# A linear-attention layer and two feed-forward layers on one core: low parts of the weights and r*k move from GpSimd to VectorE, raw chunks and attention inputs get three buffers, and the first block's gl is issued one slot part later

## The chip, the cores and the metric

The kernel runs on one core of a Trainium2 chip. The metric is the device time of one execution in microseconds, the median of three runs. Engines are named as in the profile: PE is TensorE, DVE is VectorE, ACT is ScalarE, POOL is GpSimd, SP is SyncE, which only issues transfers (SPq is its queue).

## The reference

Float32 throughout: 4 batches, 8 heads, 768 tokens, 48 channels a head. A recurrent attention makes x, then two feed-forward layers follow, each with a squared ReLU in the middle.

```python
def _attn_ref(r, k, v, w, u):
    state = np.zeros((B, H, D, D)); y = np.zeros_like(r)
    for t in range(S):
        kt, vt, rt, wt = (k[:, :, t], v[:, :, t], r[:, :, t], w[:, :, t])
        cur = np.einsum('bhd,bhe->bhde', u[None] * kt, vt)
        y[:, :, t] = np.einsum('bhd,bhde->bhe', rt, state + cur)
        state = wt[:, :, :, None] * state + np.einsum('bhd,bhe->bhde', kt, vt)
    return y

def _moe_ref(x, w_in, w_out):        # (3072, 384) @ (384, 2048), (3072, 2048) @ (2048, 384)
    h = x @ w_in
    g = np.maximum(h, 0.0) ** 2
    return g @ w_out

# reference: x = attention, tokens by channels; _moe_ref with w_in, w_out; _moe2_ref the same with its own weights
```

## The kernel before

**Products in high and low parts.** Every feed-forward product is made of three float32r products: an operand is split into a rounded high part and the rest (whi and wlo of the weights, xh and xl of x, gh and gl of the activation), and high times high, high times low and low times high are added up in PSUM.

**Slots.** Each layer goes over 7 blocks of tokens (512, 256, 256, then four of 512; in the second layer the two short ones come last), and in a block over 16 chunks f of the 2048 hidden channels. One block and one chunk make a slot; `slots` lists all 224 in order. The loop at the end of `chunked` issues for slot s, in this order: `emit_h` (nine products into h), `between(s, 0)`, `square` (ReLU and square on ScalarE), `emit_out(s - 2)` (the products of the slot two back into acc), `between(s, 1)`, `split` (gh, then gl = g - gh on VectorE). In the first block gh is made by ScalarE, later by VectorE. The schedule is manual: every engine works through its instructions in the order in which this program issues them, and semaphores hold an instruction until its operands are there and its buffer is free. A slot part is one of the two calls of `between`.

**Weights.** `Weights` turns the packed weights into whi and wlo, one chunk (128x768) at a time, 16 chunks a layer. `load` brings a raw chunk of 768 KB by SyncE's queue. `pieces` is a generator, and each call of `piece` issues one piece of it: clamp, shift, top, tail (VectorE), then whi (ScalarE) and wlo (GpSimd); ScalarE's absolute value of the next chunk (`magnitude`, `c<-raw`) is issued behind top, the load of a further raw chunk behind tail. Raw chunks have two buffers, and so have the converted words c. In the first block each slot issues three pieces in part 0 and two in part 1, and so converts the chunk that is needed two slots later. Chunks of the second layer are converted from the last block of the first layer on, at 1.6 pieces a slot part (TICKS).

**Attention.** 24 tiles of 128 tokens, each in seven steps (`Attn.steps`): 0, two scans on VectorE (G and F) and r*k on GpSimd; 1, k*G and r*F on VectorE and, on ScalarE, the squares of G and F for a range check; 2, transposes and scores on TensorE, copies on ScalarE; 3, the masked scores (ScalarE, GpSimd); 4, the state (TensorE, VectorE, ScalarE; GpSimd scales v); 5, the output y; 6, its transpose, split into xh and xl. For the first 6 tiles r*k is taken from the tile wkr (112 x 512, channels by time), for the others from rk, tokens by channels, which has a load of its own. Inputs of a tile (wkr with w, k, r, 676 KB; vn and sv) have two buffers and are loaded by SyncE's queue: wkr when step 2 of the tile two before has been issued, vn and sv behind its step 5.

**START.** Tiles 0 to 3 make the first block's x. The string START orders their steps by hand: a digit is the next step of that tile, `w` is one piece of the weights, `x` four products that nothing reads (`keep_warm`), `l` the two first raw loads. Tiles 4 and 5 have their steps in the slots of the first block (`spread`), and so on, a block ahead.

Of the kernel before, what the change touches and what calls it, by code (L numbers as in the profile page):

```python
# [19 lines left out]
T = 128  # L20
# [17 lines left out]
RAW_BUFS = 2  # L38
# [4 lines left out]
START = "lxx000x1110w1w0xw1w02w12x021323xww23w23ww23w3w3x"  # L43
# [8 lines left out]
class Attn:  # L52
# [6 lines left out]
    def __init__(self, ctx, tc, wkr, nat, u, ub, ps):  # L59
# [11 lines left out]
        self.chk = cp.tile([QR, 2 * NTILE], F32, name="chk")  # L71
# [10 lines left out]
    def load_wkr(self, i):  # L82

        if i >= NTILE:
            return
        nc = self.nc
        wkr = self.ld.tile([QR, WKR], F32, tag="wkr", name="wkr")
        rk = self.ld.tile([T, 2, H * D], F32, tag="rk", name="rk")
        cuts = (0, SW + 1, SW + 513, WKR) if i < 1 else (0, WKR)
        for lo, hi in zip(cuts, cuts[1:]):  # L90
            nc.sync.dma_start(out=wkr[:, lo:hi], in_=self.wkr_d[i, :, lo:hi])
        if i >= SUMMED_BY_PE:
            nc.sync.dma_start(out=rk, in_=self.nat_d[i, :, 0:2])
        self.wkr_t[i] = wkr, rk
# [13 lines left out]
    def load_u(self):  # L108
        self.nc.sync.dma_start(out=self.ub, in_=self.ub_d)
# [5 lines left out]
    def steps(self, i, xdst):  # L115
# [13 lines left out]
        G = self.wp1.tile([QR, SW + 1], F32, tag="G", name="G")  # L129
        F = self.wp1.tile([QR, SW + 1], F32, tag="F", name="F")  # L130
# [9 lines left out]
        r, k = rk[:, 0], rk[:, 1]  # L140
        if by_pe:
            rkT = rk.rearrange("q n d -> q (n d)")[0:QR, 0:SEG * C].rearrange("q (s t) -> q s t", s=SEG)
            nc.gpsimd.tensor_tensor(out=rkT, in0=rT, in1=kS, op=ALU.mult)
        else:
            nc.gpsimd.tensor_tensor(out=r, in0=r, in1=k, op=ALU.mult)
# [4 lines left out]
        for n, t in enumerate((G, F)):  # L150
            nc.scalar.activation(out=t[:, 1:], in_=t[:, 1:], func=AF.Square, accum_out=self.chk[:, 2 * i + n:2 * i + n + 1])
# [117 lines left out]
class Weights:  # L269


    def __init__(self, ctx, tc, packed):
# [8 lines left out]
        self.gen = None  # L281

    def load(self):
# [5 lines left out]
        self.nc.sync.dma_start(out=raw, in_=self.packed[k // KF][k % KF].bitcast(I32).rearrange("p (m w) -> p m w", w=2))  # L289
        self.raw[k] = raw  # L290

    def piece(self, end=2 * KF):

        if self.gen is None and self.begun < end:
            self.gen = self.pieces()
        if self.gen is not None and next(self.gen, 0) == 0:
# [6 lines left out]

    def pieces(self):
        nc = self.nc
# [5 lines left out]
        conv.clamp()  # L311
        yield
# [8 lines left out]
        yield  # L321
        hi, lo = self.hl[k // KF, k % KF] = tuple(self.p.tile([128, 2 * DM], F32R, tag=t, name=t) for t in ("whi", "wlo"))
        nc.scalar.copy(out=hi, in_=conv.cf)  # L323
# [403 lines left out]
```

## Time and profile before

| | us |
|---|---|
| median of three runs (lowest to highest) | 1020.34 (1018.11 to 1020.72) |
| the profiled execution | 1018.85 |
| its span, first to last instruction | 1017.0 |
| busy in the span: TensorE | 951.3 |
| VectorE | 547.3 |
| ScalarE | 473.2 |
| GpSimd | 167.2 |

The profile is one execution, read by the hardware's profiler. A row of the trace gives an instruction's engine, line, tiles, shape and duration, and the idle time of its engine before it with what ended that. Busy time is a sum over an engine's instructions. The clock is the share of full speed that was granted to TensorE: at 1.00 it runs at 2.4 GHz, at 0.5 at 1.2 GHz, and values between are a mix in time.

### The profile page before, as it was taken

How to read it: one execution, taken by the hardware profiler on the slowest of the kernel's cores; microseconds unless marked ns; L12 is line 12 of the kernel's file. 1: busy time of each engine (PE TensorE's matmuls, PEld its weight loads, DVE VectorE, ACT ScalarE, POOL GpSimd, SP SyncE). 2: the span in 40 equal slices, each digit the busy share in tenths (PEclk: the TensorE clock that was granted, in tenths of full speed). 3: DMA queues.
4: the chain of work that ended last, by engine and by line, in shares of the span. 5: the costliest groups of instructions: out<-in, count | busy, mean ns of one | idle time of the engine just before them, and what ended most of it. 6: DMA issues, size and time to landing. Idle time of an engine off the chain costs nothing.

```text
span 1017.0 us, 16836 instructions
## 1 busy us (share of the span) xinstructions
PE 951.3 (94%) x6708; PEld 830.2 (82%) x6708; DVE 547.3 (54%) x908; ACT 473.2 (47%) x923; POOL 167.2 (16%) x160
## 2 busy tenths in 40 slices
PE   6577868998999999999999999999999999999997
PEld 6565646898978888888888888999999999999996
DVE  4777667655784574655835898822323223222332
ACT  4344655555655546546454565533333333333442
POOL 2422232230323022121210222300000000000000
PEclk8757888998999999999999999999999999999999
DMA  7242443233224214123102334210010010100100
GB/s 210 91 121 93 136 136 121 83 102 102 81 86 118 79 46 126 56 78 118 32 1 73 134 123 147 84 43 11 11 42 22 14 39 11 37 6 6 47 17 19
DMA packets 28119, 73.82 MB, mean 73 GB/s; under 512 B 3616, under 2 KB 15264, under 8 KB 28032
## 3 DMA queue, kind: packets, MB, share of 16 engines
q1 hardware_dynamic: 28032, 72.66, 22.9%
q8 instruction: 54, 0.88, 0.4%
q14 instruction: 33, 0.27, 0.1%
HBM read 63.21 MB, written 9.44 MB: 71 GB/s over the span
## 4 chain that ended last, share of the span: by engine, by line
PE 64%; DVE 3%; issue 1%; DMA 1%; ACT 1%; ACTq 0%; DVEq 0%; SPq 0%
PE acc L600 30%; PE h L557 30%; PE ab L173 1%; PE ab L216 1%; DMA raw<-in_w_dram 1%; DVE gh L573 1%; DVE c L257 1%; PE ab L189 1%; PE ab L158 0%; PE ab L223 0%; DVE gl L575 0%; DVE c L260 0%; DVE c L266 0%; DVE c L263 0%; PE ab L190 0%
## 5 line engine op out<-in xcount | busy, mean ns | idle before, releaser
L557 PE MATMUL h<-xh,whi 128*128 128x512 f32 (+1 forms) x672 | 251.1, 374 | 16.8 <-ACT whi L323 16.7
L557 PE MATMUL h<-xh,wlo 128*128 128x512 f32 (+1 forms) x672 | 249.1, 371 | 8.1 <-POOL wlo L324 8.1
L557 PE MATMUL h<-xl,whi 128*128 128x512 f32 (+1 forms) x672 | 247.4, 368 | 0.0
L573 DVE CAST gh<-gf 128x512 fp32r<-128x512 f32 (+1 forms) x208 | 87.4, 420 | 296.7 <-PE acc L600 238.4
L565 ACT ACTIVATE gf<-h 128x512 f32<-128x512 f32 (+1 forms) x224 | 119.9, 535 | 272.5 <-PE h L557 270.0
L575 DVE TENSOR_TENSOR gl<-gf,gh 128x512 fp32r<-128x512 f32 (+1 forms) x224 | 161.3, 720 | 45.6 <-ACT gh L573 30.8
L557 PEld LDWEIGHTS h<-xh,whi 128*128 128x128 f32 x672 | 129.2, 192 | 38.3 <-ACT whi L323 19.7
L557 PEld LDWEIGHTS h<-xh,wlo 128*128 128x128 f32 x672 | 129.6, 193 | 32.2 <-POOL wlo L324 12.4
L557 PEld LDWEIGHTS h<-xl,whi 128*128 128x128 f32 x672 | 129.3, 192 | 16.9 <-DVE xl L226 0.3
L566 ACT ACTIVATE gf<-gf 128x512 f32<-128x512 f32 (+1 forms) x224 | 128.1, 572 | 7.1
L600 PE MATMUL acc<-whi,gh 128*128 128x384 f32 x384 | 129.4, 337 | 1.7 <-ACT o L604 1.7
L600 PE MATMUL acc<-gh,whi 128*128 128x512 f32 (+1 forms) x336 | 125.0, 372 | 5.9 <-ACT o L604 5.8
L600 PE MATMUL acc<-whi,gl 128*128 128x384 f32 x384 | 129.4, 337 | 0.0
L600 PE MATMUL acc<-wlo,gh 128*128 128x384 f32 x384 | 129.0, 336 | 0.0
L600 PE MATMUL acc<-gl,whi 128*128 128x512 f32 (+1 forms) x336 | 122.1, 363 | 0.1
L600 PE MATMUL acc<-gh,wlo 128*128 128x512 f32 (+1 forms) x336 | 121.6, 362 | 0.0
L324 POOL TENSOR_TENSOR wlo<-c,whi 128x768 fp32r<-128x768 f32 x32 | 60.9, 1902 | 175.8 <-ACT whi L323 167.2
L600 PEld LDWEIGHTS acc<-gh,whi 128*128 128x128 f32 x336 | 64.7, 193 | 17.9 <-ACT o L604 7.5
L600 PEld LDWEIGHTS acc<-whi,gh 128*128 128x128 f32 x384 | 72.3, 188 | 5.5 <-ACT o L604 2.0
L600 PEld LDWEIGHTS acc<-wlo,gh 128*128 128x128 f32 x384 | 72.2, 188 | 3.4
L600 PEld LDWEIGHTS acc<-gh,wlo 128*128 128x128 f32 x336 | 64.3, 191 | 9.8
L600 PEld LDWEIGHTS acc<-gl,whi 128*128 128x128 f32 x336 | 64.4, 192 | 9.5 <-DVE starts L132 0.3
(70 smaller groups left out, 1020.4 us busy)
## 6 DMA issues: line engine op xcount, KB each, us to landing
raw<-in_w_dram SPq DMA_DIRECT2D x32, 768.0 KB, 4.3
wkr<-in_wkr_dram SPq DMA_DIRECT2D x23, 675.9 KB, 5.1
rk<-in_nat_dram SPq DMA_DIRECT2D x18, 384.0 KB, 5.5
vn<-in_nat_dram SPq DMA_DIRECT2D x24, 192.0 KB, 2.6
sv<-in_nat_dram SPq DMA_DIRECT2D x48, 96.0 KB, 2.6
out_dram<-o SPq DMA_DIRECT2D x24, 192.0 KB, 2.0
x<-o SPq DMA_DIRECT2D x15, 256.0 KB, 2.2
xr<-x SPq DMA_DIRECT2D x12, 256.0 KB, 2.6
```

Source lines behind the costliest of these rows:

```text
L173: nc.tensor.matmul(out=scv[other[a], n, :], lhsT=kS[rows, n, :], rhs=rT[rows, n, :], start=True, stop=True)
L189: nc.tensor.matmul(out=Uv[c][0:64, p, :], lhsT=ksT[rows, p, 0:64], rhs=vn[rows, 2 * p, :], start=True, stop=True)
L216: nc.tensor.matmul(out=y[64 * c:64 * c + 64, D * h:D * h + D], lhsT=rs[rows, a, 2 * p + c, :], rhs=sv[rows, a, 2 * p + c, :], start=True, ...
L257: self.v.tensor_scalar(out=self.cf, in0=self.cf, scalar1=HIGH_WORD_MIN, scalar2=HIGH_WORD_MAX, op0=ALU.max, op1=ALU.min)
L324: nc.gpsimd.tensor_tensor(out=lo, in0=conv.cf, in1=hi.bitcast(F32), op=ALU.subtract)
L557: nc.tensor.matmul(out=h[:, 0:N], lhsT=a[:, cs], rhs=b[:, kk, 0:N], start=n == 0, stop=n == 8)
L565: nc.scalar.activation(out=g[:, 0:N], in_=h[:, 0:N], func=AF.Relu)
L566: nc.scalar.activation(out=g[:, 0:N], in_=g[:, 0:N], func=AF.Square)
L573: (nc.scalar.copy if l == j == 0 else nc.vector.tensor_copy)(out=gh[:, 0:N], in_=g[:, 0:N])
L575: nc.vector.tensor_tensor(out=gl[:, 0:N], in0=g[:, 0:N], in1=gh[:, 0:N].bitcast(F32), op=ALU.subtract)
L600: nc.tensor.matmul(out=dst, lhsT=a, rhs=c, start=f == n == 0, stop=f == KF - 1 and n == 2)
```

## The change

The low part of a chunk, `lo = c - hi`, goes from GpSimd to VectorE. It is no longer issued behind whi but in a function of its own, `cut`, which is called as the second piece of the following chunk (behind that chunk's clamp), or by a call of `piece` that finds no chunk left to begin. The number of pieces a chunk stays five: clamp, cut, shift, top, and tail with whi. `ready` counts a chunk once its low part is issued. Raw chunks get three buffers, all three loaded at the start, the first by ScalarE's queue.

r*k of the first six tiles goes from GpSimd to VectorE, behind the two scans. wkr gets three buffers; it is loaded for the tile three ahead, when step 3 has been issued, and rk, where it is loaded, for the tile two ahead. The first loads change order and queue: wkr of tile 1, ub and the first raw chunk go by ScalarE's queue, wkr of tile 2 is loaded at the start too, uB goes behind the tiles' loads.

In the first block, gl is not issued with gh in `split` but in part 0 of the next slot, behind its pieces (`rests`).

G and F lie in one tile, and one square over both replaces two; the range check has one column a tile. START has a new order: 11 pieces of the weights in place of 12, 9 `x` in place of 7. The scratch space for dynamic transfers is set to 4096.

```diff
--- before.py
+++ after.py
@@ -35,12 +35,14 @@
 RANGE_SQ = 2.0 ** 59
 
 HIGH_WORD_MIN, HIGH_WORD_MAX = 2.0 ** -15, 2.0 ** 16 * (1.875 - 2.0 ** -23)
-RAW_BUFS = 2
+RAW_BUFS = 3
+
+AHEAD = 3
 
 SUMMED_BY_PE = 6
 
 
-START = "lxx000x1110w1w0xw1w02w12x021323xww23w23ww23w3w3x"
+START = "xx000x1101wwx120w2x1w02w103x2w132wx32w3w2x3w3w3x"
 
 LEAD = 2
 
@@ -68,7 +70,7 @@
         self.ident = cp.tile([128, 128], F32, name="ident")
         self.uB = cp.tile([T, H * D], F32, name="uB")
         self.ub = cp.tile([QR, NP, 2], F32, name="ub")
-        self.chk = cp.tile([QR, 2 * NTILE], F32, name="chk")
+        self.chk = cp.tile([QR, NTILE], F32, name="chk")
         self.Sc = {}
         self.wkr_t, self.v_t = {}, {}
 
@@ -79,19 +81,24 @@
         nc.gpsimd.affine_select(out=self.ident, in_=self.ident, pattern=[[-1, 128]], base=0,
                                 channel_multiplier=1, compare_op=ALU.not_equal, fill=1.0)
 
-    def load_wkr(self, i):
+    def load_wkr(self, i, queue=None):
 
         if i >= NTILE:
             return
         nc = self.nc
-        wkr = self.ld.tile([QR, WKR], F32, tag="wkr", name="wkr")
-        rk = self.ld.tile([T, 2, H * D], F32, tag="rk", name="rk")
+        queue = queue or nc.sync
+        wkr = self.ld.tile([QR, WKR], F32, tag="wkr", name="wkr", bufs=AHEAD)
         cuts = (0, SW + 1, SW + 513, WKR) if i < 1 else (0, WKR)
         for lo, hi in zip(cuts, cuts[1:]):
-            nc.sync.dma_start(out=wkr[:, lo:hi], in_=self.wkr_d[i, :, lo:hi])
-        if i >= SUMMED_BY_PE:
-            nc.sync.dma_start(out=rk, in_=self.nat_d[i, :, 0:2])
-        self.wkr_t[i] = wkr, rk
+            queue.dma_start(out=wkr[:, lo:hi], in_=self.wkr_d[i, :, lo:hi])
+        self.wkr_t[i] = wkr, None
+
+    def load_rk(self, i):
+
+        if SUMMED_BY_PE <= i < NTILE:
+            rk = self.ld.tile([T, 2, H * D], F32, tag="rk", name="rk")
+            self.nc.sync.dma_start(out=rk, in_=self.nat_d[i, :, 0:2])
+            self.wkr_t[i] = self.wkr_t[i][0], rk
 
     def load_v(self, i):
         if i >= NTILE:
@@ -106,7 +113,9 @@
         self.v_t[i] = vn, sv
 
     def load_u(self):
-        self.nc.sync.dma_start(out=self.ub, in_=self.ub_d)
+        self.nc.scalar.dma_start(out=self.ub, in_=self.ub_d)
+
+    def load_uB(self):
         self.nc.sync.dma_start(out=self.uB, in_=self.u_d.rearrange("(o h) d -> o (h d)", o=1).to_broadcast([T, H * D]))
 
     def bank(self):
@@ -126,8 +135,8 @@
         def seg(t, o, q=slice(0, QR)):
             return t[q, 1:SW + 1].rearrange("q (s j) -> q s j", s=SEG)[:, :, o:o + C]
 
-        G = self.wp1.tile([QR, SW + 1], F32, tag="G", name="G")
-        F = self.wp1.tile([QR, SW + 1], F32, tag="F", name="F")
+        GF = self.wp1.tile([QR, 2, SW + 1], F32, tag="GF", name="GF")
+        G, F = GF[:, 0], GF[:, 1]
         aend = self.wp.tile([QR, SEG], F32, tag="aend", name="aend", bufs=4)
         nc.vector.memset(self.starts[:, 65::65], 1.0)
         nc.vector.tensor_tensor_scan(out=G[:, 1:][:, ::-1], data0=Wt[:, 1:][:, ::-1], data1=self.starts[:, 1:][:, ::-1],
@@ -137,18 +146,18 @@
         nc.vector.tensor_tensor_scan(out=F[:, 1:], data0=Wt[:, 0:SW], data1=self.starts[:, 0:SW],
                                      initial=0.0, op0=ALU.mult, op1=ALU.add)
         by_pe = i < SUMMED_BY_PE
-        r, k = rk[:, 0], rk[:, 1]
         if by_pe:
+            rk = self.ld.tile([T, 2, H * D], F32, tag="rk", name="rk")
             rkT = rk.rearrange("q n d -> q (n d)")[0:QR, 0:SEG * C].rearrange("q (s t) -> q s t", s=SEG)
-            nc.gpsimd.tensor_tensor(out=rkT, in0=rT, in1=kS, op=ALU.mult)
+            nc.vector.tensor_tensor(out=rkT, in0=rT, in1=kS, op=ALU.mult)
         else:
+            r, k = rk[:, 0], rk[:, 1]
             nc.gpsimd.tensor_tensor(out=r, in0=r, in1=k, op=ALU.mult)
             nc.gpsimd.tensor_tensor(out=r, in0=r, in1=self.uB, op=ALU.mult)
         yield
         nc.vector.tensor_tensor(out=kS, in0=kS, in1=seg(G, 1), op=ALU.mult)
         nc.vector.tensor_tensor(out=rT, in0=rT, in1=seg(F, 0), op=ALU.mult)
-        for n, t in enumerate((G, F)):
-            nc.scalar.activation(out=t[:, 1:], in_=t[:, 1:], func=AF.Square, accum_out=self.chk[:, 2 * i + n:2 * i + n + 1])
+        nc.scalar.activation(out=GF[:, :, 1:], in_=GF[:, :, 1:], func=AF.Square, accum_out=self.chk[:, i:i + 1])
         yield
         kq = self.wp.tile([T, NP * QR + H], F32, tag="ksT", name="ksT")
         ksT, q = kq[:, 0:NP * QR].rearrange("t (p q) -> t p q", p=NP), kq[:, NP * QR:]
@@ -278,22 +287,25 @@
         self.hl = {}
         self.raw = {}
         self.loaded = self.begun = self.ready = 0
-        self.gen = None
-
-    def load(self):
+        self.gen = self.whole = None
+
+    def load(self, queue=None):
         k = self.loaded
         if k >= 2 * KF:
             return
         self.loaded += 1
         raw = self.raw_p.tile([128, 2 * DM, 2], I32, tag="raw", name="raw")
-        self.nc.sync.dma_start(out=raw, in_=self.packed[k // KF][k % KF].bitcast(I32).rearrange("p (m w) -> p m w", w=2))
+        (queue or self.nc.sync).dma_start(out=raw, in_=self.packed[k // KF][k % KF].bitcast(I32).rearrange("p (m w) -> p m w", w=2))
         self.raw[k] = raw
 
     def piece(self, end=2 * KF):
 
-        if self.gen is None and self.begun < end:
+        if self.gen is None:
+            if self.begun == end:
+                self.cut()
+                return
             self.gen = self.pieces()
-        if self.gen is not None and next(self.gen, 0) == 0:
+        if next(self.gen, 0) == 0:
             self.gen = None
             self.piece(end)
 
@@ -301,8 +313,14 @@
         self.conv = ToFloat32(self.nc, self.raw.pop(k), self.tmp_p.tile([128, 2 * DM], I32, tag="c", name="c"))
         self.conv.magnitude()
 
+    def cut(self):
+        if self.whole is not None:
+            conv, hi, lo = self.whole
+            self.nc.vector.tensor_tensor(out=lo, in0=conv.cf, in1=hi.bitcast(F32), op=ALU.subtract)
+            self.whole = None
+            self.ready += 1
+
     def pieces(self):
-        nc = self.nc
         k = self.begun
         self.begun += 1
         if k == 0:
@@ -310,6 +328,8 @@
         conv = self.conv
         conv.clamp()
         yield
+        self.cut()
+        yield
         conv.shift()
         yield
         conv.top()
@@ -318,11 +338,9 @@
         yield
         conv.tail()
         self.load()
-        yield
         hi, lo = self.hl[k // KF, k % KF] = tuple(self.p.tile([128, 2 * DM], F32R, tag=t, name=t) for t in ("whi", "wlo"))
-        nc.scalar.copy(out=hi, in_=conv.cf)
-        nc.gpsimd.tensor_tensor(out=lo, in0=conv.cf, in1=hi.bitcast(F32), op=ALU.subtract)
-        self.ready = k + 1
+        self.nc.scalar.copy(out=hi, in_=conv.cf)
+        self.whole = conv, hi, lo
         yield
 
     def done(self):
@@ -485,10 +503,15 @@
     block_of = [j for j, n in enumerate(BLOCKS[0]) for _ in range(n // T)]
 
     A.load_wkr(0)
+    A.load_wkr(1, nc.scalar)
     A.load_u()
     A.load_v(0)
-    A.load_wkr(1)
+    W.load(nc.scalar)
+    A.load_wkr(2)
     A.load_v(1)
+    A.load_uB()
+    for _ in range(RAW_BUFS - 1):
+        W.load()
     A.consts()
 
     xs = {}
@@ -512,8 +535,9 @@
             gens[i] = A.steps(i, lambda: xdst(i))
         next(gens[i])
         seen[i] += 1
-        if seen[i] == 3:
-            A.load_wkr(i + 2)
+        if seen[i] == 4:
+            A.load_wkr(i + AHEAD)
+            A.load_rk(i + 2)
         elif seen[i] == NSTEP - 1:
             A.load_v(i + 2)
 
@@ -533,10 +557,7 @@
 
     keep_warm(9)
     for what in START:
-        if what == "l":
-            for _ in range(RAW_BUFS):
-                W.load()
-        elif what == "w":
+        if what == "w":
             W.piece()
         elif what == "x":
             keep_warm(4)
@@ -570,10 +591,18 @@
         N = BLOCKS[l][j]
         g = gs[l, j, f]
         gh = g_p.tile([128, 512], F32R, tag="gh", name="gh")
-        (nc.scalar.copy if l == j == 0 else nc.vector.tensor_copy)(out=gh[:, 0:N], in_=g[:, 0:N])
         gl = g_p.tile([128, 512], F32R, tag="gl", name="gl")
-        nc.vector.tensor_tensor(out=gl[:, 0:N], in0=g[:, 0:N], in1=gh[:, 0:N].bitcast(F32), op=ALU.subtract)
         gs[l, j, f] = gh, gl
+        late = l == j == 0
+        (nc.scalar.copy if late else nc.vector.tensor_copy)(out=gh[:, 0:N], in_=g[:, 0:N])
+
+        def rest():
+            nc.vector.tensor_tensor(out=gl[:, 0:N], in0=g[:, 0:N], in1=gh[:, 0:N].bitcast(F32), op=ALU.subtract)
+
+        if late:
+            rests.append(rest)
+        else:
+            rest()
 
     x2 = [dram.tile([128, 3, n], F32, name=f"x2_{j}") for j, n in enumerate(BLOCKS[0])]
     slots = [(l, j, f) for l in range(2) for j in range(len(BLOCKS[l])) for f in range(KF)]
@@ -648,8 +677,9 @@
         if s < L0:
             if j == 0:
                 for _ in range(3 - part):
-                    if W.begun < min(KF, f + LEAD + 1) or W.gen is not None:
-                        W.piece(min(KF, f + LEAD + 1))
+                    W.piece(min(KF, f + LEAD + 1))
+            if part == 0 and rests:
+                rests.pop()()
             if j + 1 < len(BLOCKS[0]):
                 if (f, part) == (0, 0):
                     plan[:] = spread(j + 1, 2 * KF)
@@ -661,6 +691,7 @@
     plan = []
     bad = []
     due = [0]
+    rests = []
     for s in range(total + 2):
         if s < total:
             l, j, f = slots[s]
@@ -714,7 +745,7 @@
     import concourse.bacc as bacc
     from concourse.bass_utils import run_bass_kernel_spmd
 
-    nc = bacc.Bacc("TRN2", target_bir_lowering=False, num_devices=1)
+    nc = bacc.Bacc("TRN2", target_bir_lowering=False, num_devices=1, dynamic_dma_scratch_size=4096)
     arrays, args = {}, []
     for name, a in lay_out(**inputs).items():
         arrays[f"in_{name}_dram"] = a
```

## Rows read from the trace of the kernel before

**Rows 1.** Windows by stage: stretch, length, busy time of each engine, clock, DMA share, GB/s.

```profile
0.00:68.00 68.00, 43.76 (x519) 40.52 (x519) 41.15 (x62) 29.21 (x59) 22.69 (x28) 0.70 0.50 145
68.00:183.00 115.00, 90.26 (x493) 67.95 (x492) 82.89 (x95) 60.76 (x103) 37.24 (x25) 0.84 0.38 123
183.00:302.00 119.00, 111.40 (x1216) 103.03 (x1215) 80.08 (x165) 67.23 (x167) 26.53 (x32) 0.97 0.30 88
302.00:1017.00 715.00, 705.89 (x4485) 618.65 (x4485) 343.20 (x588) 315.98 (x596) 80.75 (x76) 1.00 0.17 55
```

**Rows 2.** Waits of TensorE from 340 us to the end: total, times, longest.

```profile
PE acc L600 <- ACT o L604: 1.7, 1, 1.7
```

**Rows 3.** Timeline of TensorE: the first product of block 0 (start, duration).

```profile
67.94 0.77 PE L557 MATMUL h<-xh,whi 128*128 128x512 f32 x1
```

**Rows 4.** Groups on VectorE, 68 to 183 us: busy, mean ns of one | idle before.

```profile
L575 DVE TENSOR_TENSOR gl<-gf,gh 128x512 fp32r<-128x512 f32 x15 | 26.5, 1764 | 28.1 <-ACT gh L573 28.1
...
L266 DVE SCALAR_TENSOR_TENSOR c<-raw,c 128x768 int32<-128x768 int32 x14 | 13.3, 952 | 0.3
L257 DVE TENSOR_SCALAR c<-c 128x768 f32<-128x768 f32 x13 | 9.5, 728 | 0.0
...
L148 DVE TENSOR_TENSOR wkr<-wkr,G 112x512 f32<-112x512 f32 x2 | 1.4, 686 | 0.0
```

**Rows 5.** Timeline of one slot of block 0, all engines but TensorE.

```profile
126.55 0.96 DVE L266 SCALAR_TENSOR_TENSOR c<-raw,c 128x768 int32<-128x768 int32 x1
...
127.64 0.81 ACT L323 CAST whi<-c 128x768 fp32r<-128x768 f32 x1
128.36 0.62 ACT L573 CAST gh<-gf 128x512 fp32r<-128x512 f32 x1
...
128.53 1.81 POOL L324 TENSOR_TENSOR wlo<-c,whi 128x768 fp32r<-128x768 f32 x1 [4.62 <-ACT whi L323]
...
129.01 1.88 DVE L575 TENSOR_TENSOR gl<-gf,gh 128x512 fp32r<-128x512 f32 x1 [1.50 <-ACT gh L573]
```

**Rows 6.** Timeline at 601 us, second-layer weights: VectorE and GpSimd.

```profile
601.14 0.69 DVE L575 TENSOR_TENSOR gl<-gf,gh 128x512 fp32r<-128x512 f32 x1
...
601.72 1.84 POOL L324 TENSOR_TENSOR wlo<-c,whi 128x768 fp32r<-128x768 f32 x1 [4.42 <-ACT whi L323]
601.75 2.23 DVE L257 TENSOR_SCALAR c<-c 128x768 f32<-128x768 f32 x1
```

**Rows 7.** Timeline of VectorE in START.

```profile
3.86 1.24 DVE L133 TENSOR_TENSOR_SCAN G<-wkr,starts 112x520 f32<-112x520 f32 x1 [2.23 <-DMA wkr<-in_wkr_dram]
...
8.53 0.69 DVE L149 TENSOR_TENSOR wkr<-wkr,F 112x512 f32<-112x512 f32 x1
...
12.91 2.30 DVE L133 TENSOR_TENSOR_SCAN G<-wkr,starts 112x520 f32<-112x520 f32 x1 [3.68 <-DMA wkr<-in_wkr_dram]
...
24.06 0.56 DVE L257 TENSOR_SCALAR c<-c 128x768 f32<-128x768 f32 x1 [5.87 <-ACT c L254]
...
30.82 3.47 DVE L133 TENSOR_TENSOR_SCAN G<-wkr,starts 112x520 f32<-112x520 f32 x1
...
59.02 2.26 DVE L197 TENSOR_TENSOR Sp<-Sn,aend 112x192 f32<-112x192 f32 x1
...
62.07 0.36 DVE L197 TENSOR_TENSOR Sp<-Sn,aend 112x192 f32<-112x192 f32 x1 [0.33 <-ACT sv L202]
```

**Rows 8.** Groups on ScalarE, 68 to 183 us.

```profile
L254 ACT ACTIVATE c<-raw 128x768 f32<-128x768 f32 x14 | 12.9, 922 | 34.2 <-DMA raw<-in_w_dram 29.4 <-POOL wlo L324 4.7
L323 ACT CAST whi<-c 128x768 fp32r<-128x768 f32 x14 | 11.5, 822 | 8.4 <-DVE c L266 6.7 <-DVE starts L132 1.5
```

**Rows 9.** Groups on GpSimd, 68 to 183 us.

```profile
L324 POOL TENSOR_TENSOR wlo<-c,whi 128x768 fp32r<-128x768 f32 x14 | 25.7, 1835 | 75.4 <-ACT whi L323 75.4
```

**Rows 10.** DMA issues on the page: KB each, median us to landing.

```profile
raw<-in_w_dram SPq DMA_DIRECT2D x32, 768.0 KB, 4.3
```

**Rows 11.** Window of six microseconds in block 0, columns as in rows 1.

```profile
84.00:90.00 6.00, 5.75 (x16) 4.18 (x14) 5.79 (x9) 2.07 (x3) 0.90 (x1) 0.60 0.00 0
```

## The prediction

> **What bounds the kernel now.** I read the stage windows first. From 302 us to the end TensorE is busy for 705.9 of 715 us at clock 1.00, and between 183 and 302 for 111.4 of 119 [rows 1]; in the last two thirds it waits once, 1.7 us [rows 2]. Nothing that VectorE, GpSimd or the queues do there can move the end by more than a few microseconds. The time that can be won lies ahead of 183 us: the START order (0 to 68, TensorE busy 43.8, clock 0.70) and block 0 of the first layer (68 to 183, busy 90.3 of 115, clock 0.84) [rows 1]. Since the stages behind are full of TensorE work that depends on nothing but these two, what block 0 ends earlier, the kernel ends earlier.
>
> Next, what holds block 0. Its first product starts at 67.94 [rows 3]. Each slot needs one converted chunk. VectorE is busy for 82.9 us and idle for 32.1 [rows 1]; 28.1 of those 32.1 stand ahead of gl, waiting for ScalarE's gh [rows 4]. The timeline of one slot shows why: tail ends at 127.51, whi runs to 128.45, gh behind it to 128.98, only then gl at 129.01 and, behind gl, the next clamp [rows 5]. So gl, last in its slot, puts VectorE through a ScalarE round trip in every slot. Meanwhile GpSimd's low part runs from 128.53 to 130.34, and gl, begun at 129.01, ends at 130.89, after 1.88 us [rows 5]. The same gl without GpSimd takes 0.69; a clamp begun 0.03 us behind a low part takes 2.23 and ends 0.42 after it [rows 6], where a free one takes 0.56 [rows 7]. I read this as VectorE standing still while GpSimd's low part runs. The mean gl in block 0, 1.764 [rows 4], is thus 1.07 too long. ScalarE besides waits 29.4 us for raw chunks [rows 8], and its whi queues behind that.
>
> **Block 0, summed on VectorE.** From its 82.9 us busy [rows 1]:
> - gl without GpSimd beside it: 15 x (1.764 - 0.69) = -16.1 [rows 4, 6].
> - clamp likewise: 13 x (0.728 - 0.56) = -2.2 [rows 4, 7].
> - The low parts come to VectorE: chunks 1 to 15, 15 instructions. No 128x768 subtraction of VectorE stands in the trace. Between the 512-element gl (0.69, as if size were free) and GpSimd's own 1.835 [rows 9] I take 0.952, that of tail, also 768 elements from two SBUF operands [rows 4]: +14.3. The bounds would make this 10.4 or 27.5.
> - r*k of tiles 4 and 5, 112x512 from SBUF as the product with G: 2 x 0.686 = +1.4 [rows 4].
> - START has one piece less (11 for 12), so the shift of chunk 2 falls here: +0.6, a clamp's time.
>
> That is 80.9 busy. Waits: a low part needs whi, which ends 0.94 us after tail [rows 5]; the next clamp covers 0.58 of it, so 14 x 0.36 = 5.0 remain. gl now runs behind clamp, low part and shift of the next slot, over 2 us after tail, while whi and gh are done 1.47 after it [rows 5]: its 28.1 us go. The other idle time, 32.1 - 28.1 = 4.0, I leave. Sum 89.9. The last low part now comes a piece later than its whi, with products behind it: +2. So 92 for 115, **23 us less**.
>
> Can TensorE follow? 90.3 busy at clock 0.84 [rows 1] is 90.3 x 0.84 = 76 at full clock (an estimate), and at 0.84 itself just under 92. It fits, narrowly.
>
> Raw chunks: a load is issued behind tail of chunk k and takes 4.3 us [rows 10]. With two buffers it is wanted one slot later, with three two slots later; at 92 / 16 = 5.7 us a slot that is 2 x 5.7 - 0.95 = 10.4 us; the 29.4 us wait [rows 8] should vanish. Behind a waiting load on SyncE's queue stand all later ones; a tile's load that waits over 6 us would make one raw chunk late. Since wkr is now loaded one step later for a tile further ahead, it finds its buffer freer. I cost the loads at nothing; uncovered, the bound is the 29.4.
>
> One Square for G and F does the same elements in one instruction less; ScalarE is busy for 60.8 of 115 us [rows 1], so nothing. In START, though, tile 1's scan now waits for both halves, some 0.6 us (estimated from whi, 0.822 for 768 elements [rows 8]).
>
> **Weights of the second layer.** 16 low parts come to VectorE, +0.95 each, and the clamp beside them loses 2.23 - 0.56 = 1.67 [rows 6, 7]. TensorE hides both: it does not wait there [rows 2]. Zero; without the cover, 16 x 0.95 = 15 us.
>
> **START.** Tile 1's scan began at 12.91 after 3.68 us of waiting for its load [rows 7]; that load now stands first on ScalarE's queue instead of ninth on SyncE's. It can begin once tile 0 is done: its last product, begun at 8.53, ended at 9.22 [rows 7]; with its r*k on VectorE (0.69) and its Square (about 1.2) that is 11.1, -1.8. GpSimd's r*k and low parts no longer stretch the scans of tiles 1 and 2 (2.30 and 3.47, against 1.24) and one state product (2.26 against 0.36): -5.2 [rows 7]. VectorE takes on four r*k and a low part and loses a shift: 4 x 0.69 + 0.95 - 0.56 = +3.2. That makes -3.8. The new order puts tile 2's scan right behind the first clamp, where it came 6.8 us later (24.06 to 30.82 [rows 7]); some of this returns as waiting for TensorE, and I take 3 of 6.2. **START: 7 us less**, bounds 2 to 13: the lower without the reordering's 3 and with the delay of the next paragraph, the upper with all of the 6.2 and half of the 5.87 us that the first clamp waited.
>
> Against it: two transfers now start together. At the stage's 145 GB/s [rows 1] the 228 KB of tile 0's first piece (112 partitions of 521 floats) are 1.6 us, the most by which tile 1's load can delay it. The Trainium skill (DMA: Bandwidth & Descriptors, "Issuing engines are not separate DMA queues") speaks against the second queue: transfers of different issuers interleave on the same 16 DMA engines and only issue time is saved. By that, START gains 5.4 and not 7; no row of this trace has two issuers.
>
> **Sum.** 1018.85 (the profiled execution, span 1017.0) - 23 - 7 = **989 us**. The median shown, 1020.34, lies 1.5 above, inside the spread of the three runs.
>
> **Rivals.**
> - *TensorE's clock takes part of it.* At a mean of 0.75, between the 0.70 of START and the 0.84, its work is 76 / 0.75 = 101 us, not 92: 998 us. For it: short waits now come in every slot. Against: while TensorE is slow it is itself late, and waits stop.
> - *The clock stays down all through block 0*, the slower side. At the 0.60 of 84 to 90 us [rows 11], 76 / 0.60 = 127, +12, less START's 7: 1024 us. It decides where 76 / c exceeds 115 + 7, at c under 0.62. Against: that stretch is 6 us of the 115. The Trainium skill (TensorE: Matmul & The Clock Gate, "HAM oscillation") tells of kernels that wait in every iteration and start each one cold; by it this rival would hold, and the 0.84 of block 0 [rows 1] bears it out only in part.
> - *The round trip only moves*, from gl to the low part or to raw chunks behind held loads: half of the 28.1 stays, block 0 gains 9: 1003 us.
> - *Better than the sum.* START gains 12, and whi and leftover waits overlap with attention (5.0 + 4.0), as do two stretched scans (2): 1018.85 - 34 - 12 = 973.
> - *GpSimd isn't what stretches VectorE*: the change would not do what it says. The 18.3 of gl and clamp and the 5.2 of START stay: 1013 us; with low parts at 1.835 another 13, 1026. Against: [rows 6].
>
> **Chances.** Forecast 0.48; clock at 0.75 0.17; round trip moved 0.12; better 0.11; GpSimd innocent 0.05, half of it slower; clock down 0.07, some of it no change. Three runs tell 0.3% from no change here, about 3 us. Faster 0.88, same 0.04, slower 0.08. The forecast's own range is 982 to 996; the range for 8 in 10 reaches to the clock, the moved round trip and the better case: 973 to 1008.
>
> **What would show it.** Right: gl near 0.69 in block 0 and no wait for gh; no long clamps; low parts near 0.95, each behind a wait of some 0.4 for whi; ScalarE's waits for raw gone; tile 1's scan near 11 us; first product near 61 and block 0 over near 153; behind it the same row of stages, shifted. Wrong: clock under 0.75 in block 0, TensorE waiting for low parts over 2 us a slot, ScalarE held by raw, or a later stage that lets TensorE idle.

## The result, and the profile after

The changed kernel takes 994.12 us (median of four runs, 992.73 to 996.80); four runs of the kernel before have a median of 1019.34, and the ratio to it is 0.9755, 95% interval 0.9728 to 0.9783. One of the four runs of e3 below took 1522.64 us at a granted clock of 0.555 and isn't part of its ratio. The profiled execution took 992.73 us, its span is 990.9, which is 26.1 less than before.

The windows, cut where block 0 begins and ends, in the columns of [rows 1]:

```profile
0.00:64.66 64.66, 50.14 (x534) 46.86 (x535) 39.39 (x66) 27.52 (x50) 13.07 (x22) 0.65 0.58 174
64.66:157.43 92.77, 80.45 (x495) 62.96 (x495) 78.84 (x113) 60.34 (x99) 10.98 (x10) 0.91 0.46 153
157.43:276.00 118.57, 110.70 (x1213) 102.48 (x1212) 78.33 (x162) 65.29 (x151) 25.24 (x30) 0.97 0.30 88
276.00:990.00 714.00, 706.49 (x4488) 619.00 (x4486) 336.06 (x608) 315.17 (x575) 49.20 (x60) 1.00 0.17 53
```

Block 0 begins with its first product and ends with the first product of block 1, which has 256 columns. In the timeline of TensorE of the changed kernel:

```profile
64.66 0.77 PE L578 MATMUL h<-xh,whi 128*128 128x512 f32 x1
```

```profile
157.43 0.28 PE L578 MATMUL h<-xh,whi 128*128 128x256 f32 x1
```

The second boundary of the kernel before:

```profile
183.26 0.28 PE L557 MATMUL h<-xh,whi 128*128 128x256 f32 x1
```

So START took 67.94 us [rows 3] and now takes 64.66: 3.3 us less. Block 0 took 183.26 - 67.94 = 115.3 and now takes 157.43 - 64.66 = 92.8: 22.5 less. Together that is 25.8 of the 26.1; the stages behind only moved. No wait of TensorE is left from 300 us to the end, where [rows 2] had one of 1.7.

The groups on VectorE in block 0, answering to [rows 4]:

```profile
L319 DVE TENSOR_TENSOR wlo<-c,whi 128x768 fp32r<-128x768 f32 x15 | 14.5, 965 | 5.9 <-ACT whi L342 5.9
...
L275 DVE SCALAR_TENSOR_TENSOR c<-raw,c 128x768 int32<-128x768 int32 x14 | 14.1, 1007 | 0.5
L600 DVE TENSOR_TENSOR gl<-gf,gh 128x512 fp32r<-128x512 f32 x15 | 11.4, 758 | 0.6 <-ACT gh L597 0.6
...
L266 DVE TENSOR_SCALAR c<-c 128x768 f32<-128x768 f32 x13 | 7.2, 555 | 4.5 <-ACT c L263 4.5
...
L152 DVE TENSOR_TENSOR rk<-wkr 112x512 f32<-112x512 f32 x2 | 1.3, 666 | 0.0
```

gl takes 0.758 on average for 1.764, and of its 28.1 us of waiting for gh 0.6 are left; a clamp takes 0.555 for 0.728. The low part is new: 15 of 0.965 us, with 5.9 us of waiting for whi. Clamps wait 4.5 us for the absolute value. One slot, all engines but TensorE, answering to [rows 5]:

```profile
91.14 0.96 DVE L275 SCALAR_TENSOR_TENSOR c<-raw,c 128x768 int32<-128x768 int32 x1
...
92.02 0.55 DVE L266 TENSOR_SCALAR c<-c 128x768 f32<-128x768 f32 x1
92.13 0.83 ACT L342 CAST whi<-c 128x768 fp32r<-128x768 f32 x1 [1.45 <-DVE c L275]
...
92.87 0.61 ACT L597 CAST gh<-gf 128x512 fp32r<-128x512 f32 x1
93.00 0.96 DVE L319 TENSOR_TENSOR wlo<-c,whi 128x768 fp32r<-128x768 f32 x1 [0.43 <-ACT whi L342]
...
94.34 0.69 DVE L600 TENSOR_TENSOR gl<-gf,gh 128x512 fp32r<-128x512 f32 x1
```

The clamp now runs beside whi, the low part waits 0.43 us for whi instead of gl waiting for gh, and gl comes behind clamp, low part and shift, when gh has been done for 0.86 us. This slot is 4.79 us long (whi to whi, 92.13 to 96.92); the mean over block 0 is 92.8 / 16 = 5.8. ScalarE in block 0, answering to [rows 8]:

```profile
L263 ACT ACTIVATE c<-raw 128x768 f32<-128x768 f32 x14 | 12.5, 895 | 1.5 <-DVE wlo L319 1.5
L342 ACT CAST whi<-c 128x768 fp32r<-128x768 f32 x14 | 11.6, 831 | 18.1 <-DVE c L275 18.1
```

The 29.4 us of waiting for raw chunks are gone; whi waits for tail, so that VectorE now leads. The second layer's weights on VectorE, answering to [rows 6]:

```profile
568.93 0.55 DVE L266 TENSOR_SCALAR c<-c 128x768 f32<-128x768 f32 x1
...
569.86 0.69 DVE L600 TENSOR_TENSOR gl<-gf,gh 128x512 fp32r<-128x512 f32 x1
570.47 0.95 DVE L319 TENSOR_TENSOR wlo<-c,whi 128x768 fp32r<-128x768 f32 x1
```

The clamp of 2.23 us is one of 0.55, and the low part takes its 0.95 on VectorE. TensorE's clock still falls in places of block 0, here in the window that answers to [rows 11]:

```profile
86.00:92.00 6.00, 3.77 (x9) 2.71 (x10) 5.50 (x8) 3.31 (x5) 0.00 (x0) 0.61 0.39 134
```

Over the whole of block 0 it was 0.91 for 0.84 (windows above), and TensorE was busy for 80.5 us. Last, START on VectorE, answering to [rows 7]:

```profile
6.90 1.24 DVE L142 TENSOR_TENSOR_SCAN GF<-wkr,starts 112x520 f32<-112x520 f32 x1 [5.27 <-DMA wkr<-in_wkr_dram]
...
13.43 1.24 DVE L142 TENSOR_TENSOR_SCAN GF<-wkr,starts 112x520 f32<-112x520 f32 x1 [1.21 <-ACT GF L160]
...
23.30 0.56 DVE L266 TENSOR_SCALAR c<-c 128x768 f32<-128x768 f32 x1 [5.00 <-ACT c L263]
...
23.92 1.24 DVE L142 TENSOR_TENSOR_SCAN GF<-wkr,starts 112x520 f32<-112x520 f32 x1
...
58.40 0.74 DVE L206 TENSOR_TENSOR Sp<-Sn,aend 112x192 f32<-112x192 f32 x1
```

Tile 0's first scan begins at 6.90, not at 3.86; tile 1's at 13.43, not at 12.91; tile 2's at 23.92, right behind the first clamp, not at 30.82. No scan with GpSimd's r*k beside it is left, and the state product of 2.26 us takes 0.74. GpSimd's masks and products still lengthen a few instructions of VectorE: the product of 0.74 is one, the second scan of tile 2 another (2.31 us, shown with e5).

### The profile page after: what moved, and what is told of

Read it like the earlier page. It is cut to its first block, busy times and chain, and to the rows that moved or that the text cites. A ratio compares the mean times of both kernels' runs of the same rounds, so it can differ in the third digit from the quotient of the medians.

```text
span 990.9 us, 16785 instructions
## 1 busy us (share of the span) xinstructions
PE 947.8 (96%) x6724; PEld 831.3 (84%) x6724; DVE 532.6 (54%) x946; ACT 468.3 (47%) x875; POOL 98.5 (10%) x122
## 4 chain that ended last, share of the span: by engine, by line
PE 82%; DVE 9%; ACT 5%; issue 2%; DVEq 0%; ACTq 0%
PE h L578 37%; PE acc L629 36%; PE ab L225 3%; PE ab L182 2%; DVE GF L142 1%; ACT GF L160 1%; PE ab L232 1%; DVE gl L600 1%; DVE GF L146 1%; PE ab L167 1%; PE ab L198 1%; ACT whi L342 1%; DVE Sp L206 1%; DVE c L275 1%; DVE wlo L319 1%
## 5 line engine op out<-in xcount | busy, mean ns | idle before, releaser
L578 PE MATMUL h<-xh,wlo 128*128 128x512 f32 (+1 forms) x672 | 245.6, 365 | 0.8 <-DVE wlo L319 0.8
L597 DVE CAST gh<-gf 128x512 fp32r<-128x512 f32 (+1 forms) x208 | 82.2, 395 | 301.4 <-PE acc L629 266.4
L600 DVE TENSOR_TENSOR gl<-gf,gh 128x512 fp32r<-128x512 f32 (+1 forms) x224 | 144.6, 646 | 18.1 <-ACT gh L597 2.9
L629 PEld LDWEIGHTS acc<-whi,gl 128*128 128x128 f32 x384 | 72.0, 188 | 0.0
```

Of the source, the lines that this page charges most:

```text
L578: nc.tensor.matmul(out=h[:, 0:N], lhsT=a[:, cs], rhs=b[:, kk, 0:N], start=n == 0, stop=n == 8)
L597: (nc.scalar.copy if late else nc.vector.tensor_copy)(out=gh[:, 0:N], in_=g[:, 0:N])
L600: nc.vector.tensor_tensor(out=gl[:, 0:N], in0=g[:, 0:N], in1=gh[:, 0:N].bitcast(F32), op=ALU.subtract)
L629: nc.tensor.matmul(out=dst, lhsT=a, rhs=c, start=f == n == 0, stop=f == KF - 1 and n == 2)
```

## The experiments

For every kernel: the ratio to runs of the kernel before that were made along with it, its 95% interval, and from the timeline of TensorE in its one profiled execution the end of START and the length of block 0. In block 0 the changed kernel and e4 execute the same instructions; their 92.77 and 92.75 us tell how closely two profiles agree there.

| kernel | ratio | interval | START, us | block 0, us |
|---|---|---|---|---|
| before | 1 | | 67.9 | 115.3 |
| changed | 0.9755 | 0.9728 to 0.9783 | 64.7 | 92.8 |
| e1: changed, low parts on GpSimd | 0.9808 | 0.9781 to 0.9834 | 66.5 | 97.1 |
| e2: changed, gl at once | 0.9868 | 0.9841 to 0.9895 | 64.1 | 105.5 |
| e3: changed, two raw buffers | 0.9758 | 0.9717 to 0.9799 | 63.7 | 93.1 |
| e4: changed, first loads on one queue | 0.9704 | 0.9675 to 0.9734 | 61.6 | 92.8 |
| e5: changed, r*k on GpSimd | 0.9742 | 0.9720 to 0.9764 | 65.9 | 91.0 |
| e6: before, low parts on VectorE | 0.9879 | 0.9856 to 0.9902 | 66.0 | 108.8 |
| e7: before, gl late | 0.9880 | 0.9850 to 0.9910 | 68.3 | 104.3 |
| e9: before, both of these | 0.9743 | 0.9721 to 0.9765 | 66.2 | 91.4 |
| e8: e4, two G and F tiles, two raw buffers | 0.9724 | 0.9707 to 0.9740 | 61.1 | 93.6 |
| e10: e4, r*k of tiles 4 and 5 on GpSimd | 0.9699 | 0.9679 to 0.9720 | 61.2 | 91.5 |
| e11: e8 and e10 together | 0.9716 | 0.9697 to 0.9734 | 61.5 | 93.5 |
| e12: changed, tile 1's load cut | 0.9728 | 0.9703 to 0.9752 | 62.5 | 92.2 |

**e1, the low parts' engine alone.**

```diff
-            self.nc.vector.tensor_tensor(out=lo, in0=conv.cf, ...)
+            self.nc.gpsimd.tensor_tensor(out=lo, in0=conv.cf, ...)
```

> The changed kernel (994 us) with only the low parts put back on GpSimd, in their new place behind the next chunk's clamp. If the lengthened instructions of VectorE in block 0 were GpSimd's doing, VectorE loses the low part (0.965) and its wait for whi (about 0.4), but stands still for some 1.3 to 1.7 us of each low part, in the shift or gl now: shift or gl near 2.2 in block 0, 0.3 to 0.5 us more a slot, 1000 us (997 to 1004). If GpSimd was not the cause: shift and gl keep 0.55 and 0.68, VectorE saves 1.4 us a slot, and the time is near 994 or falls to some 985.

1001.17 us; block 0 is 4.3 us longer though VectorE is rid of 15 instructions. VectorE's groups in block 0, and two instructions of its timeline:

```profile
L600 DVE TENSOR_TENSOR gl<-gf,gh 128x512 fp32r<-128x512 f32 x16 | 29.2, 1824 | 7.7 <-ACT gh L597 7.3
...
L266 DVE TENSOR_SCALAR c<-c 128x768 f32<-128x768 f32 x14 | 8.6, 613 | 4.8 <-ACT c L263 4.8
```

```profile
113.76 1.85 POOL L319 TENSOR_TENSOR wlo<-c,whi 128x768 fp32r<-128x768 f32 x1 [1.82 <-ACT whi L342]
...
114.17 1.99 DVE L600 TENSOR_TENSOR gl<-gf,gh 128x512 fp32r<-128x512 f32 x1 [0.36 <-ACT gh L597]
```

It is gl, now the instruction that meets the low part, that stretches, from 0.758 to 1.824; in the timeline it starts 0.41 us behind GpSimd's low part and ends 0.55 behind its end. The theory holds in place, and the size is somewhat less than the 2.2 expected; the rival (time at 994 or less) falls. Another rival is that TensorE was slowed by the later low parts: in block 0 it waits 8.0 us for GpSimd's low parts here and 0.8 for VectorE's in the changed kernel. But VectorE is idle for 97.1 - 83.3 = 13.8 us here and for 92.8 - 78.8 = 14.0 there, so the 4.3 us lie in VectorE's busy time, and not in waits that TensorE passed on. The Trainium skill (SBUF — State Buffer, "SBUF: two separate sides") gives a cause: VectorE and GpSimd share a port pair under an exclusive lock, and a VectorE instruction with two SBUF inputs, such as gl, that finds it taken by a GpSimd instruction which reads SBUF stands still until it is free. The end 0.55 us behind the other's end, where gl alone takes 0.69, agrees with that; the trace does not show the port.

**e2, the place of gl alone.**

```diff
-        if late:
-            rests.append(rest)
-        else:
-            rest()
+        rest()
```

> The changed kernel with gl of the first block issued in its own slot again, directly behind gh. If the round trip through ScalarE was the large wait of block 0, VectorE waits some 1.5 us behind tail for gh in each of 13 slots and saves the 0.4 of the low part: 1.1 us a slot, about 15 us: 1009 us (1004 to 1013), with 15 to 25 us of idle time ahead of gl for gh. If the round trip only mattered together with GpSimd's low part, the time stays within 4 us of 994.

1006.55 us, block 0 12.7 us longer. The two groups on VectorE:

```profile
L319 DVE TENSOR_TENSOR wlo<-c,whi 128x768 fp32r<-128x768 f32 x14 | 13.8, 983 | 0.9 <-ACT whi L342 0.9
...
L600 DVE TENSOR_TENSOR gl<-gf,gh 128x512 fp32r<-128x512 f32 x15 | 10.4, 691 | 22.2 <-ACT gh L597 22.1
```

gl keeps its 0.691 us and waits 22.1 us for gh; the low part saves 5 of its 5.9. The round trip costs by itself, without GpSimd's low part.

**e3, the third raw buffer alone.**

```diff
-RAW_BUFS = 3
+RAW_BUFS = 2
```

> The changed kernel with two raw buffers for three (two raw chunks loaded at the start). If the third buffer is needed: a raw chunk lands 4.3 us behind tail and is wanted about 4 us behind it, whi queues behind it on ScalarE; 0.4 us a slot and more where a tile's loads stand ahead on SyncE's queue: 999 us (996 to 1005), with 10 to 30 us of ScalarE waiting for raw. If the shorter slot hides the load even so, 994 within 2.

0.9758, the changed kernel's ratio; block 0 is 0.3 us longer, START 1.0 shorter. ScalarE's group in block 0:

```profile
L263 ACT ACTIVATE c<-raw 128x768 f32<-128x768 f32 x14 | 12.7, 908 | 12.0 <-DMA raw<-in_w_dram 8.2 <-DVE c L272 1.7 <-DVE wlo L319 1.5
```

8.2 us of waiting for raw come back, less than expected, and clamps wait 1.5 us longer for ScalarE in all (6.0 for 4.5). The theory that the third buffer is needed falls.

**e4, the first loads.**

```diff
-    A.load_wkr(1, nc.scalar)
+    A.load_wkr(1)
...
-    W.load(nc.scalar)
+    W.load()
```

> The changed kernel with tile 1's wkr and the first raw chunk on SyncE's queue again, in the same order of issue; nothing else moved. If the second queue cost START its missing 4 us (the first scan began at 6.90 where it began at 3.86 before), the first scan is back near 3.9, tile 1's scan comes at 11 or earlier instead of 13.4, the first product of block 0 at 61.5 to 63 instead of 64.7, and the kernel takes 991 to 992. If START is held by what stands behind the first tiles (TensorE's transposes and scores, ScalarE's copies), the scans move but the first product does not: 994 within 1.

989.92 us. Scans of tiles 0, 1 and 2 on VectorE, and block 0's first product:

```profile
4.27 1.24 DVE L142 TENSOR_TENSOR_SCAN GF<-wkr,starts 112x520 f32<-112x520 f32 x1 [2.63 <-DMA wkr<-in_wkr_dram]
...
10.37 1.24 DVE L142 TENSOR_TENSOR_SCAN GF<-wkr,starts 112x520 f32<-112x520 f32 x1 [1.21 <-ACT GF L160]
...
20.87 1.24 DVE L142 TENSOR_TENSOR_SCAN GF<-wkr,starts 112x520 f32<-112x520 f32 x1
```

```profile
61.61 0.77 PE L578 MATMUL h<-xh,whi 128*128 128x512 f32 x1
```

Tile 0's scan is 2.63 us earlier than in the changed kernel, tile 1's 3.06, tile 2's 3.05, the first product 3.05: the delay of tile 0's load went through START undiminished.

**e5, r*k alone.**

```diff
-            nc.vector.tensor_tensor(out=rkT, ...)
+            nc.gpsimd.tensor_tensor(out=rkT, ...)
```

> The changed kernel (994 us) with r*k of the first six tiles back on GpSimd. If GpSimd's two-operand instructions hold up VectorE, the scans of tiles 1 to 3 and the products behind them lengthen again (2 to 3.5 us against 1.24), more than the 0.67 that VectorE saves a tile: START 1 to 4 us longer, 996 to 998. If not, VectorE saves 6 x 0.67 and the time is 991 to 994.

0.9742, the changed kernel's ratio within both intervals. START is 1.2 us longer. The second scan of tile 2 is stretched as expected. In the changed kernel it is long too: in both it begins while a mask of GpSimd runs, and ends 1.1 us behind the product with v that GpSimd does next; in e5 r*k stands between the two. First e5, then the changed kernel:

```profile
26.90 3.53 DVE L146 TENSOR_TENSOR_SCAN GF<-wkr,starts 112x520 f32<-112x520 f32 x1
...
28.51 0.82 POOL L200 TENSOR_TENSOR vn<-vn,ksT 128x384 f32<-128x384 f32 x1
```

```profile
25.92 2.31 DVE L146 TENSOR_TENSOR_SCAN GF<-wkr,starts 112x520 f32<-112x520 f32 x1
...
26.30 0.82 POOL L200 TENSOR_TENSOR vn<-vn,ksT 128x384 f32<-128x384 f32 x1
```

Block 0 is 1.8 us shorter; why is not shown. The move of r*k brought nothing that can be measured in the kernel's time; the expected 2 to 4 us were a miss.

**e6, e7 and e9, the two main parts alone and together, in the kernel before.** e6:

```diff
-        nc.gpsimd.tensor_tensor(out=lo, in0=conv.cf, ...)
+        nc.vector.tensor_tensor(out=lo, in0=conv.cf, ...)
```

> The kernel before (1020 us) with its low parts on VectorE in their old place, directly behind whi; one part of the change alone. If standing still behind GpSimd costs VectorE 16 to 18 us in block 0 and a low part 0.95: the low part waits 0.94 for whi, gl then finds gh ready and takes 0.69, about 0.8 us a slot less, with the clamps 13 us, and a little in START: 1007 us (1003 to 1010). If the waits, not GpSimd, were the cost, VectorE only gets more to do: 1020 or up to 1030.

1009.35 us. VectorE's groups in block 0:

```profile
L324 DVE TENSOR_TENSOR wlo<-c,whi 128x768 fp32r<-128x768 f32 x14 | 13.4, 958 | 26.9 <-ACT whi L323 26.9
...
L575 DVE TENSOR_TENSOR gl<-gf,gh 128x512 fp32r<-128x512 f32 x15 | 10.9, 726 | 0.6 <-ACT gh L573 0.6
```

gl is short (0.726) and no longer waits, but the low part in front of it waits 26.9 us for whi, twice what I had reckoned. e7 has the new `split` and `rests` of the change, and nothing else:

```diff
-        nc.vector.tensor_tensor(out=gl[:, 0:N], ...)
+        if late:
+            rests.append(rest)
+        else:
+            rest()
...
+            if part == 0 and rests:
+                rests.pop()()
```

> The kernel before with gl of the first block one slot part later, low parts still on GpSimd; the other part alone. If the round trip is the cost and GpSimd's low part then falls on clamp and shift, which stretch: block 0 near 98 us for 115: 1003 us (999 to 1008). If raw chunks with two buffers set the pace behind it (29.4 us of waiting before), it gains less than 8: 1012 or more.

1008.63 us, between the two expectations. VectorE's and ScalarE's groups:

```profile
L579 DVE TENSOR_TENSOR gl<-gf,gh 128x512 fp32r<-128x512 f32 x16 | 27.3, 1709 | 10.4 <-ACT gh L576 10.4
```

```profile
L254 ACT ACTIVATE c<-raw 128x768 f32<-128x768 f32 x14 | 12.7, 909 | 32.0 <-DMA raw<-in_w_dram 25.4 <-POOL wlo L324 6.3 <-POOL rk L143 0.3
```

gl waits 10.4 us where it waited 28.1, but takes 1.709, since GpSimd's low part meets it in its new place too. e9 adds `cut` to e7, with the pieces of the change:

```diff
-        nc.gpsimd.tensor_tensor(out=lo, in0=conv.cf, ...)
-        self.ready = k + 1
+        self.whole = conv, hi, lo
...
         conv.clamp()
         yield
+        self.cut()
+        yield
```

> The kernel before with both: low parts on VectorE behind the next clamp, and gl late; START's order, loads, two raw buffers and r*k as before. If these two make block 0's gain, it takes 93 to 95 us for 115, and with a little of START the time is 996 (993 to 1000), less than the sum of the two parts alone would give, since each alone takes part of the same wait away. If the third raw buffer, the moved r*k or the new loads are needed for it, 1003 or more.

994.11 us, 0.9743: the whole gain of the change, with START's order, the loads, two raw buffers and r*k as before.

```profile
L310 DVE TENSOR_TENSOR wlo<-c,whi 128x768 fp32r<-128x768 f32 x14 | 13.4, 956 | 3.5 <-ACT whi L333 3.5
L588 DVE TENSOR_TENSOR gl<-gf,gh 128x512 fp32r<-128x512 f32 x16 | 11.4, 714 | 2.5 <-ACT gh L585 2.5
```

Alone the parts bring 1.21% and 1.20%, together 2.57%. I had expected less than the sum; the kernel's time, with intervals of 0.2 to 0.3% to either side, can't tell 2.57 from 2.41. Block 0 can: it is 6.5 us shorter in e6, 11.0 in e7 and 23.9 in e9, more than the 17.5 of the two. Each alone leaves a cost of the other standing (the low part's wait of 26.9 in e6, gl's 1.709 in e7), and both go only together.

**e8, e10, e11, on top of e4.** e8 has the first two edits, e10 the third, e11 all of them.

```diff
-        GF = self.wp1.tile([QR, 2, SW + 1], F32, tag="GF", name="GF")
+        GF = self.wp1.tile([QR, 2, SW + 1], F32, tag="GF", name="GF", bufs=2)
...
-RAW_BUFS = 3
+RAW_BUFS = 2
...
-            nc.vector.tensor_tensor(out=rkT, ...)
+            (nc.vector if i < 4 else nc.gpsimd).tensor_tensor(out=rkT, ...)
```

> The kernel with the first loads on one queue (990 us) and two buffers for the tile of G and F; raw chunks go back to two buffers to make room. Tile 1's first scan waited 1.2 us for tile 0's square, which reads both halves of the one tile. If that wait is passed on, the first product of block 0 comes 1.2 us earlier (near 60.4) and the kernel takes 989. If START is held behind it by ScalarE's copies or TensorE, the scan moves and the first product does not: 990.

> The kernel with the first loads on one queue (990 us) with r*k on VectorE for the four tiles of START alone and on GpSimd for tiles 4 and 5, whose steps lie in block 0. With r*k on GpSimd for all six, block 0 took 1.8 us less and START 1.2 more. If both come from where r*k stands, block 0 takes 91 for 92.75, START stays at 61.6, and the kernel takes 988. If that difference was chance, 990.

> Both of the last two together: 987 us if each brings what its theory says, 990 if neither does.

In e8 tile 1's scan no longer waits for the square, but for its own load:

```profile
9.66 1.24 DVE L142 TENSOR_TENSOR_SCAN GF<-wkr,starts 112x520 f32<-112x520 f32 x1 [0.64 <-DMA wkr<-in_wkr_dram]
```

START is 0.5 us shorter and block 0 0.8 longer; 0.9724 is no gain. e10 took 987.84 us; the profile has its block 0 at 91.5, near the expected 91, yet its interval and e4's overlap for the most part, so r*k's place is not shown to matter. e11, at 990.82 and with 93.5 us in block 0, brings neither. e10's interval lies below that of the changed kernel, so that e10 beats both kernels; e4's reaches 0.0006 into it, and its earlier first product says the same.

**e12, why the second queue delays tile 0.**

```diff
-        cuts = (0, SW + 1, SW + 513, WKR) if i < 1 else (0, WKR)
+        cuts = (0, SW + 1, SW + 513, WKR) if i < 2 else (0, WKR)
```

> The changed kernel with tile 1's wkr, still on ScalarE's queue, cut into the three pieces that tile 0's has (rows of some 2 KB for 6.2 KB); issue costs two more issues on ScalarE's queue. If the two queues take turns row by row, tile 0's first piece (2 KB rows) gets a quarter of the transfer rate beside whole rows and half of it beside cut ones: the first scan, at 6.90 in the changed kernel and 4.27 with one queue, comes between 5.0 and 5.7, the first product of block 0 near 63.4. If the delay does not depend on the size of the rows (the shared rate alone, or the start of a second queue), the first scan stays at 6.7 to 7.0 and the time at 994.

992.31 us, first product at 62.5. The first scan, and an issue on ScalarE's queue:

```profile
5.31 0.36 ACTq L298 DMA_DIRECT2D raw<-in_w_dram  x1
5.39 1.24 DVE L142 TENSOR_TENSOR_SCAN GF<-wkr,starts 112x520 f32<-112x520 f32 x1 [3.76 <-DMA wkr<-in_wkr_dram]
```

5.39 lies in the range of the row theory: with short rows beside it, tile 0's first piece is 1.5 us earlier. The Trainium skill (DMA: Bandwidth & Descriptors, "Queues, rings and completion order") states that each DMA engine takes turns between its queues a packet at a time; the direction agrees. The first raw chunk, behind tile 1 on that queue, was issued at 5.31 instead of 1.76, and could be a second cause. What each queue had moved by 4.0 us speaks against it (packets, MB, share of 16 engines; q1 is SyncE's queue, q10 ScalarE's). First the changed kernel, then e12:

```profile
q1 hardware_dynamic: 73, 0.15, 24.7%
q10 hardware_dynamic: 53, 0.33, 23.2%
```

```profile
q1 hardware_dynamic: 129, 0.25, 28.2%
q10 hardware_dynamic: 103, 0.20, 21.4%
```

In the changed kernel none of the small packets of ub, which stands ahead of the raw chunk, had been moved by then, and the 0.33 MB are less than half of tile 1's 676 KB. So tile 0's queue was behind (0.15 MB for 0.25) while it shared with tile 1's long rows alone. A run with only the raw chunk moved was not made.

## Why the prediction was right, and where a term was off

**Block 0** was forecast at 92 us and took 92.8, from terms that came out nearly as worked out. gl went from 1.764 to 0.758 (forecast 0.69; two of the 15 still meet a mask or a product of GpSimd and take 1.14 and 1.32), the clamp to 0.555 (0.56), a low part to 0.965 (0.952), r*k to 0.666 (0.686). VectorE was busy for 78.8 (80.9). Low parts wait 5.9 for whi (5.0). The rest of its idle time, 92.8 - 78.8 - 5.9 = 8.1, had been set at 4.0 and 2; more than half of it, 4.5, is the clamp waiting for the absolute value, which I had not named. That the sum came so near is in part luck: busy time was 2.1 too high and idle time 3.0 too low. The busy time was too high although its terms together were not: durations were added up, but an instruction can begin before the one ahead of it has ended (in the slot above tail ends at 92.10 and the clamp begins at 92.02), and busy time counts such a stretch once. The durations of all VectorE's groups in block 0 add up to 85.8 before and 84.3 after, only 1.5 less, where busy time fell by 4.1. e1, e2 and e9 show the two mechanisms to be what the prediction called them.

**GpSimd as the cause** was read from two durations [rows 6] and is shown by e1: same place, other engine, and gl stretches again.

**START** is the term that was mis-sized: forecast 7 us less, measured 3.3. The step that failed is "1.6 us, the most by which tile 1's load can delay it": the first scan came 3.0 later. I had priced the piece by itself at the stage's mean rate and then left even that out of the sum; e4 shows the delay to be the second queue's, and e12 that it is smaller when that queue's rows are short. Tile 1's scan, forecast near 11, came at 13.43, in e4 at 10.37. With one queue START gains 6.3, close to the 7 of the remaining terms; of those only r*k was tried apart, 1.2 in e5. The Trainium skill's rule that was weighed there (DMA: Bandwidth & Descriptors, "Issuing engines are not separate DMA queues") had the right sign: the second issuer's transfers came between tile 0's and delayed them. All queues together moved no less for it, 241 GB/s over the first 12 us for 215 in e4, but the bytes that came sooner were not those of tile 0. The 5.4 that followed with it rested on the same 1.6, and was too high too.

**Raw chunks.** The wait of 29.4 us did vanish, as forecast, but not by the third buffer: in e9 12.7 us (two buffers) stand ahead of ScalarE's absolute values and block 0 is as short. Before, ScalarE waited for raw because loads are issued behind tail, and tail was late; it was slack and not cost, and the 29.4 was no price for it.

**The clock** rose rather than fell: 0.91 for 0.84 in block 0, with eight waits of TensorE for whi and wlo left, 12.3 us in all and the longest 3.5. The two rivals by which it has a mean of 0.75 (998) or stays down (1024) are out: waits in half of the slots did not bring that about. The rival of a moved round trip has its truth in the 5.9 us of low parts behind whi, a fifth of what gl had waited. The second layer cost nothing, as forecast.

## What to carry to other kernels

Where an instruction of VectorE takes two or three times its usual time, look at what GpSimd runs beside it and whether the two end together: moving GpSimd's instruction to VectorE can pay although VectorE is the busier engine. Then look at what the last instruction of a repeated part waits for on another engine; issuing it one part later lets the next part's work cover the round trip. Try two such edits together too: each alone can leave the cost of the other standing, as in block 0 here. Idle time of an engine that only follows another's lateness (raw chunks here) is no gain to be had, and at the start of a kernel a second queue can delay the one transfer on which everything hangs.

## What was unexpected of the hardware

A transfer on a second queue held up a smaller one by more than an equal share of bytes would: tile 0's first piece, 228 KB, landed 2.9 us after its issue before and 3.3 in e4, 6.0 in the changed kernel beside tile 1's 676 KB on ScalarE's queue, and 4.5 in e12, where those came in three pieces. By 4.0 us the packets of the two queues were nearer to each other (73 and 53 in the changed kernel, 129 and 103 in e12) than the bytes of the changed kernel (0.15 and 0.33 MB).

An instruction of VectorE that GpSimd held up ended a nearly constant time behind GpSimd's, a little less than it takes alone, as if it had begun its work only then: a clamp 0.42 us (0.56 alone) [rows 6, 7], gl in e1 0.55 (0.69), a scan 1.1 (1.24) in e5 and in the changed kernel, behind the last of several GpSimd instructions in a row.
